# Cross-covariance attention folded into a gated FFN: an earlier load, smaller first folds, sums begun from 1e-9, and five trailing tiles

## Chip, cores, metric

One core of one Trainium2 chip. The metric is the device time of the kernel in microseconds (us), the median of several executions. Each kernel was also run once under the profiler; the span of an execution, from its first instruction to its last, is 1.7 to 2.2 us shorter than its timed duration. All executions used here are of the fast state, with a granted TensorE clock of 0.995 to 1.0, so no difference below is one of clock.

Engines in the profile: PE is TensorE, PEld its weight loads, DVE VectorE, ACT ScalarE, POOL GpSimd, SP SyncE. A name with q, such as SPq, is that engine's sequencer, which issues DMAs.

## The reference, cut

```python
# q, k, v: (4, 5824, 256) f32; tau = 1.0; w1, w2: (256, 1024); w3: (1024, 1024); w_out: (1024, 256)
qn = q / (norm(q, axis=1) + 1e-6)
kn = k / (norm(k, axis=1) + 1e-6)
a  = exp(kn.T @ qn / tau - max)              # 256 x 256 for each of 4 batches
a /= a.sum(-1) + 1e-9
x  = v @ a                                   # (4*5824, 256)
out = ((x @ w1) * (x @ w2)) @ w3 @ w_out     # (23296, 256) f32
```

## The kernel before

The kernel never forms `x`. For each batch it *folds* the softmax matrix into the weights, `Wf = a @ [w1 | w2]`, and once, for all batches, forms `W = w3 @ w_out`. What is left for every 512 rows of `v` and every 128 of the 1024 hidden columns (a "unit") is two products a and b of `v` with `Wf` (four 512-wide matmuls, on transposed `v`), a copy of a by ACT, a multiplication by DVE, and four 256-wide matmuls with `W`, which trail by two units. A batch has eleven chunks of 512 rows and a narrow one of 192 (128 rows, and 64 *left rows*). The q·k products G, squares, softmax and folds of the next batch are slipped between the units of the current one, at places that a clock in the program decides.

Batch 0 has no units to hide in: load of q and k, squares and G on TensorE, exponentials, sums and folds come before the first product.

```python
def sum_mm(c2):
    if c2 == 0:
        st["sum"] = psum.tile(...)
        ...
    for c1 in range(CT):
        nc.tensor.matmul(m[:, c1:c1+1], lhsT=st["e"][:, c2, c1*P:(c1+1)*P], rhs=ones_b,
                         start=(c1 == 0 and c2 == 0), stop=...)
    if c2 == CT - 1:
        nc.vector.tensor_scalar_add(rs, m[:, :CT], 1e-9)
        nc.vector.reciprocal(rs, rs)

def fold(i, ...):        # two 512-wide matmuls into a PSUM bank, evacuated with scale rs
    ...                  # by ACT (even i) or DVE (odd i)

# one later batch: (cost, time on the program's clock, work)
return (
    [(0.0, 0.0, norms), (0.0, 6.0, k_row)]      # norms: all-reduce over partitions, on GpSimd
    ...                                         # ACT and DVE: norms, scaling, exponentials
    + [(0.2, 15.5, sums)]
    + [(0.43, 16.5 + 0.85 * i, lambda i=i: fold(i)) for i in range(8)]
)

# loads while batch 0 is computed: (tensor, batch, piece, clock); t0..t1 spreads the q.k products
moves = [("v", 0, 3, 29.0), ("qk", 1, 0, 38.0), ..., ("v", 1, 2, 116.0), ("qk", 2, 0, 126.0)]
t0, t1 = 57.0, 115.5
```

All loads are issued by GpSimd and cast f32 to bf16 on the way.

## Time and profile before

| | before |
|---|---|
| median time (range) | 572.96 us (572.88 to 575.41), 3 runs |
| profile's span | 571.7 us |
| TensorE busy | 98% of the span |
| last large piece of k landed | 31.48 us |
| first product a | 40.69 us |

The table is read with the prediction below, which shows the page and the start. Columns of the timeline: start in us, duration, engine, line, operation, output and inputs, count, and in brackets the idle time before and its releaser.

Timeline of the kernel before, three lines from 47 to 167 us:

```profile
48.05 0.61 PE L132 MATMUL tr_I-620_621<-ident_b,v 128*128 128x128 bf16 x8
...
162.53 3.19 POOL L258 PARTITION_ALL_REDUCE tot<-acc  x1
...
166.12 0.42 ACT L279 ACTIVATE kr<-tot 128x256 f32<-128x256 f32 x1
```

The first is TensorE's transposing of v's second piece, which landed at 44.78: 3.3 us of slack. The all-reduce for batch 1 ends at 165.72, and ACT wants its result at 166.12: 0.4 us of slack. (In a second profile of the same kernel, b_again2 below, it is 164.54 and 165.61: 1.1 us.) No line has a wait, and so no wait told of the small margin.

Windows of the kernel before, 3 to 4 us (busy time of each engine with counts, then clock, DMA share, GB/s):

```profile
3.00:4.00 1.00, 1.00 (x4) 0.37 (x3) 0.00 (x0) 0.00 (x0) 1.00 (x3) 1.00 0.75 125
```

DMA is at 0.75 in the ramp, at 1.11 in each of the two microseconds after it.

### The profile page before, as it was taken

Reading aid. Unit: us, or ns where it says so; the run is one execution under the profiler, and the core shown is the slowest. Engines: PE = TensorE matmul, PEld = TensorE weight load, DVE = VectorE, ACT = ScalarE, POOL = GpSimd, SP = SyncE. Lnnn points to the kernel's source line nnn. Section 1 sums busy time; section 2 is a strip of 40 time slices with the busy share of each in tenths; the row PEclk is TensorE's granted clock in tenths of the full one; section 3 lists DMA queues with packets and bytes.
Section 4 is the critical chain, followed back from the end, with each engine's and each line's share of the span. In section 5 each row is a group of like instructions: output and inputs, shape, how many; then the busy total and the mean of one; then the engine's idle time right before and its main releaser. Section 6 shows DMA issues by size and latency. Waiting matters only on the chain.

```text
span 571.7 us, 10102 instructions
## 1 busy us (share of the span) xinstructions
PE 559.4 (98%) x3750; PEld 354.5 (62%) x3750; DVE 377.4 (66%) x612; ACT 337.7 (59%) x624; POOL 83.3 (15%) x164
## 2 busy tenths in 40 slices
PE   7789999999999999999999999999999999999997
PEld 4655576776666666666666666666665666666665
DVE  1047744788977567887776667778876656565564
ACT  0046644777856567776766567767766554454453
POOL 5250020303030111121030012031120000000000
PEclk9999999999999999999999999999999999999999
DMA  8999959869685697495661595665640325221011
GB/s 163 211 187 208 184 104 240 170 149 242 140 183 118 123 204 150 94 192 121 145 144 72 99 215 123 140 136 126 175 110 38 85 73 148 63 63 75 38 72 58
DMA packets 74560, 76.93 MB, mean 135 GB/s; under 512 B 54160, under 2 KB 58256, under 8 KB 74512
## 3 DMA queue, kind: packets, MB, share of 16 engines
q0 software_dynamic: 15504, 39.46, 39.3%
q1 hardware_dynamic: 58784, 36.64, 22.2%
q8 instruction: 29, 0.48, 0.3%
q10 hardware_dynamic: 224, 0.20, 0.1%
q14 instruction: 19, 0.16, 0.1%
HBM read 78.91 MB, written 23.86 MB: 180 GB/s over the span
## 4 chain that ended last, share of the span: by engine, by line
PE 92%; DMA 5%; DVE 1%; ACT 1%; POOL 1%; issue 0%; ACTq 0%; POOLq 0%
PE o L479 28%; PE a L438 27%; PE b L438 27%; PE G L188 5%; DMA k<-in_k_dram 5%; PE fold L349 2%; PE w L596 1%; ACT as L444 0%; ACT kr L279 0%; POOL k L109 0%; POOL q L109 0%; DVE abs L453 0%; PE sqk L221 0%; DVE vT L136 0%; DVE abs L455 0%
## 5 line engine op out<-in xcount | busy, mean ns | idle before, releaser
L453 DVE TENSOR_TENSOR abs<-as,b 128x512 bf16<-128x512 bf16 x336 | 230.5, 687 | 141.4 <-ACT as L444 130.3
L444 ACT CAST as<-a 128x512 bf16<-128x512 f32 (+1 forms) x384 | 216.1, 563 | 176.9 <-DVE abs L453 90.2
L438 PEld LDWEIGHTS <-Wf 128*128 128x128 bf16 x1536 | 149.2, 98 | 102.0 <-issue 1.9
L479 PE MATMUL o<-W_sb,abs 128*128 128x256 bf16 x1376 | 209.6, 273 | 0.1
L438 PE MATMUL a<-vT,Wf 128*128 128x512 bf16 x704 | 209.4, 379 | 0.2
L438 PE MATMUL b<-vT,Wf 128*128 128x512 bf16 x704 | 209.3, 379 | 0.0
L479 PEld LDWEIGHTS <-abs 128*128 128x128 bf16 x1376 | 134.5, 98 | 81.6 <-DVE abs L455 0.3
L197 DVE TENSOR_TENSOR acc<-acc,sq 128x1024 f32<-128x1024 f32 x66 | 80.4, 1219 | 0.4 <-ACT sq L185 0.3
L188 PE MATMUL G<-k,q 128*128 128x256 bf16 x276 | 49.9, 273 | 0.0
L185 ACT ACTIVATE sq<-q 128x512 f32<-128x512 bf16 x66 | 41.8, 634 | 0.0
L185 ACT ACTIVATE sq<-k 128x512 f32<-128x512 bf16 x66 | 41.6, 630 | 0.0
L426 POOL COPY gate_t<-abs 1x1 bf16<-1x1 bf16 x39 | 13.9, 355 | 167.7 <-DVE abs L453 167.0
L500 DVE COPY osb<-o 128x512 f32<-128x512 f32 x44 | 30.1, 685 | 0.7 <-PE o L479 0.7
L430 POOL COPY gate_t<-vT 1x1 bf16<-1x1 bf16 x17 | 4.4, 258 | 169.3 <-DMA vT<-v 134.0
L188 PEld LDWEIGHTS <-q 128*128 128x128 bf16 x276 | 27.0, 98 | 3.1
L499 ACT COPY osb<-o 128x512 f32<-128x512 f32 x44 | 25.8, 586 | 3.8 <-PE o L479 1.8
L279 ACT ACTIVATE kr<-row 128x256 f32<-128x256 f32 x1 | 0.4, 385 | 31.6 <-PE row L267 31.6
L109 POOL DMA_DIRECT2D q<-in_q_dram x29 | 15.7, 541 | 13.2 <-DMA k<-in_k_dram 6.0
L349 PE MATMUL fold<-w,e 128*128 128x512 bf16 x64 | 17.0, 380 | 0.5 <-DVE vT L136 0.4
L356 ACT ACTIVATE Wf<-fold,rs 128x512 bf16<-128x512 f32 x16 | 10.9, 688 | 8.1 <-PE fold L349 6.4
L244 DVE TENSOR_TENSOR dk<-sqk,ident 128x256 f32<-128x256 f32 x1 | 0.4, 425 | 21.3 <-PE sqk L221 21.3
L109 POOL DMA_DIRECT2D k<-in_k_dram x25 | 13.8, 551 | 3.7 <-DMA k<-in_k_dram 1.9
(89 smaller groups left out, 240.4 us busy)
## 6 DMA issues: line engine op xcount, KB each, us to landing
out_dram<-osb SPq DMA_DIRECT2D x44, 512.0 KB, 3.1
k<-in_k_dram POOLq DMA_DIRECT2D x19, 512.0 KB, 8.5
v<-in_v_dram POOLq DMA_DIRECT2D x19, 512.0 KB, 5.2
q<-in_q_dram POOLq DMA_DIRECT2D x18, 512.0 KB, 6.6
w_wout<-in_moe_w_dram POOLq DMA_DIRECT2D x1, 2048.0 KB, 23.6
k<-in_k_dram POOLq DMA_DIRECT2D x4, 320.0 KB, 9.9
v<-in_v_dram POOLq DMA_DIRECT2D x4, 320.0 KB, 5.4
q<-in_q_dram POOLq DMA_DIRECT2D x4, 256.0 KB, 12.0
```

What stands on the lines that cost most here:

```text
L109: nc.gpsimd.dma_start(out=pieces[nm, n, pi][:, lo:hi, :], in_=qk_main[nm, n][0][:, pi * PIECE + lo : pi * PIECE + hi, :])
L185: nc.scalar.activation(out=dst[:, :, part, :], in_=src[:, o : o + 2, :], func=AF.Square)
L188: nc.tensor.matmul(G[:, ct, :], lhsT=qt[:, i, ct * P : (ct + 1) * P], rhs=kt[:, i, :], start=(pr == 0 and part == 0 and ct == 0), stop=(pr ...
L197: nc.vector.tensor_add(accs[n], accs[n], sqs[0])
L349: nc.tensor.matmul(st["fold", i], lhsT=st["e"][:, c2, c1 * P : (c1 + 1) * P], rhs=w12[:, c2, w, h * 512 : (h + 1) * 512], start=(c2 == 0), ...
L426: nc.gpsimd.tensor_copy(gate_t, last_ab[0][:1, :1])
L438: nc.tensor.matmul(t[:, :n], lhsT=Wf[b][:, ct, w, j * P : (j + 1) * P], rhs=rhs_of(b, c, ct), start=(ct == 0), stop=(ct == CT - 1),)
L444: nc.scalar.copy(a_sb[:, :n], tiles[0][:, :n])
L453: nc.vector.tensor_mul(ab, a_sb, tiles[1])
L479: nc.tensor.matmul(tl[h][:, o, :], lhsT=lhsT, rhs=W_sb[:, j, :], start=(j == 0 and o == 0), stop=(j == FT - 1 and (small or o == 1)), skip ...
L499: nc.scalar.copy(o[:, 0:2, :], tl[0])
L500: nc.vector.tensor_copy(o[:, 2:4, :], tl[1])
```

## The change

Its intent: (1) the load of q and k starts earlier, with half of the first pieces over SP as f32, cast by DVE and ACT; (2) before the first product only a quarter of the fold is done, in 256-wide pieces (for this the weights come in three parts, behind v's first half); (3) the small add of 1e-9 on the way from sums to reciprocal goes, as the sums' bank is begun with 1e-9 by a tiny f32 matmul; (4) in later batches sums and folds come later on the clock and wider apart; (5) q and k of the next batch are loaded ahead of late v pieces, and their products come earlier; (6) in the very last chunk outputs trail by five units, left rows first.

```diff
+LAG_END = 5
+    tiny = consts.tile([1, P], F32)
+    nc.vector.memset(tiny, 1e-9)
 ...
+        def sum_start():
+            st["sum"] = psum.tile(...)
+            nc.tensor.matmul(st["sum"][:, :CT], lhsT=tiny, rhs=ones_pp[:1, :CT], start=True, stop=False, ...)
 ...
-                    start=(c1 == 0 and c2 == 0), stop=...
+                    start=False, stop=...
-                nc.vector.tensor_scalar_add(rs, m[:, :CT], 1e-9)
-                nc.vector.reciprocal(rs, rs)
+                nc.vector.reciprocal(rs, m[:, :CT])
 ...
+        def quarter_mm(lo, c1, c2):      # 256-wide folds of both weights, lo = 0 before the first product
+            ...
-            + [(0.2, 15.5, sums)]
-            + [(0.43, 16.5 + 0.85 * i, lambda i=i: fold(i)) for i in range(8)]
+            + [(0.2, 16.5, sums)]
+            + [(0.43, 17.5 + 1.1 * i, lambda i=i: fold(i)) for i in range(8)]
 ...
-        for s, lhsT in enumerate(lhs):
+        for s, lhsT in reversed(list(enumerate(lhs))) if small else enumerate(lhs):
 ...
-    busy(14)
-    load_piece("k", 0, 0, (half,))
-    load_piece("q", 0, 0, (half,))
+    busy(10)
+    for nm in "kq":
+        ...
+        nc.sync.dma_start(out=raw[nm], in_=qk_main[nm, 0][0][:, :half, :])
+        load_part(nm, 0, 0, half, PIECE)
 ...
-            for i in range(2):
-                at(1.5 + 0.6 * i, 0.43, soft0[5 + i])
+            at(0.5, 0.87, soft0[5])                       # second quarter
+            for i in range(4):
+                at((1.7, 2.6, 3.5, 3.9)[i], 0.43, soft0[7 + i])
 ...
-            moves = [("v", 0, 3, 29.0), ("qk", 1, 0, 38.0), ("qk", 1, 1, 43.0), ("v", 0, 4, 50.0), ("qk", 1, 2, 58.0)]
-            ...
-            t0, t1 = 57.0, 115.5
+            moves = [("qk", 1, 0, 29.0), ("v", 0, 3, 30.0), ("qk", 1, 1, 43.0), ("qk", 1, 2, 47.0), ("v", 0, 4, 53.0)]
+            ...
+            t0, t1 = 54.0, 113.0
 ...
-            t0, t1 = 16.0, 104.0
+            t0, t1 = 16.0, 98.0
 ...
-                while w_ready[0] and len(pend) > LAG and npop < 2:
+                lag = LAG_END if b == B - 1 and c == NCH - 1 else LAG
+                while w_ready[0] and len(pend) > lag and npop < 2:
```

## The prediction

> **What bounds the kernel now.** I read the page first, then the chain that ended last, the waits of TensorE, and the timeline of three places: the start, one stage where weights are folded, and the end.
>
> ```profile
> span 571.7 us, 10102 instructions
> PE 559.4 (98%) x3750; PEld 354.5 (62%) x3750; DVE 377.4 (66%) x612; ACT 337.7 (59%) x624; POOL 83.3 (15%) x164
> PE 92%; DMA 5%; DVE 1%; ACT 1%; POOL 1%; issue 0%; ACTq 0%; POOLq 0%
> L438 PE MATMUL a<-vT,Wf 128*128 128x512 bf16 x704 | 209.4, 379 | 0.2
> ```
>
> TensorE carries 92% of the chain and DMA 5%; the vector and scalar engines have a third of the span free. The 379 ns of one matmul is not its price: the timeline puts the start of each pair of 128x512 matmuls 0.43 us after the last pair, so one costs 0.216 us of TensorE, a 256-wide one 0.108. I took every matmul's start and subtracted columns/2400 us from the distance to the next. From 36 to 570 us this leaves 517.4 us of columns and 13.1 us of excess. Plain stretches have 0.16 us of excess in 10 us, some 8.5 in all. What is above that lies in few places: 0.5 us at 39 us (first folds), 3.3 us in the three later fold stages (1.0 near 175, 0.7 near 305, 1.6 near 440), 0.6 us at the end. Nothing between them can be won by waiting less. So three places are left: the load of q and k before the first product, the fold stages, the end.
>
> The start (timeline of 0 to 42 us; columns: start, duration, engine, line, operation, output and inputs, idle before and its releaser):
>
> ```profile
> 1.22 1.23 POOL L109 DMA_DIRECT2D k<-in_k_dram  x2 [0.78 <-POOLq L692]
> 31.53 0.84 PE L221 MATMUL sqk<-k 128*128 128x128 bf16 x12 [0.18 <-DMA k<-in_k_dram]
> 37.02 0.20 PE L328 MATMUL sum<-ones_b,e 128*128 128x1 bf16 x2 [1.25 <-ACT e L318]
> 39.82 1.04 PE L349 MATMUL fold<-w,e 128*128 128x512 bf16 x4 [0.35 <-DVE vT L136]
> 40.69 0.59 PE L438 MATMUL a<-vT,Wf 128*128 128x512 bf16 x2
> ```
>
> The first DMA is issued at 1.22 us and lands at 5.19; the last large piece of k lands at 31.48; from there a chain of squares, row sum, four activations, scaling and exponentials leads to the sums at 37.02, and folds fill TensorE until the first product at 40.69. In between DMA is the limit:
>
> ```profile
> 12.00:14.00 2.00, 1.08 (x14) 0.58 (x11) 0.00 (x0) 0.00 (x0) 0.34 (x1) 1.00 1.07 215
> ```
>
> DMA share is full at 215 GB/s written as bf16, that is 430 GB/s read as f32, with TensorE half idle (1.08 of 2.00). The later fold stage and the end:
>
> ```profile
> 438.29 1.65 PE L349 MATMUL fold<-w,e 128*128 128x512 bf16 x6
> 440.07 0.59 PE L438 MATMUL a<-vT,Wf 128*128 128x512 bf16 x2
> ...
> 567.45 0.28 PE L479 MATMUL o<-W_sb,abs 128*128 128x256 bf16 x1
> 568.60 0.53 ACTq L497 DMA_DIRECT2D out_dram<-oleft  x1
> ```
>
> Three folds in a row (1.29 us of columns) take 1.78 us until the next a, because each must be evacuated to free its bank. The last main output matmul starts at 567.45; copy, issue and landing take 4.2 us more.
>
> **What the Trainium skill says.** "TensorE: Matmul & The Clock Gate", section "Back-to-back issue gap", gives N/2.4 + 2.5 ns warm as the isolated gap, 216 ns for 512; the trace agrees with that (0.43 us for two), and not with the 131 ns that the section gives as sustained. "DMA: Bandwidth & Descriptors", section "Latency and other measured facts", gives the first byte of a transfer issued by SP or ACT as about 600 ns against about 1 us from GpSimd. The trace shows less of a difference: GpSimd's first issue at 1.22 has its first packet at 2.60 (1.38 us), ACT's store issued at 568.17 has its first at 569.51 (1.34 us). So I count only the earlier issue. The same page, section "SWDGE vs HWDGE vs iDMA", says that a cast during DMA needs GpSimd; the change accordingly loads f32 by SP and casts on DVE and ACT.
>
> **The change part by part.** The listing of both programs by engine gives the counts.
>
> *Start of the load.* Half of the first k and q pieces now come over SP as f32, which needs no descriptor work of GpSimd. ACT and DVE start at 0.72 and 0.80 us, so I take SP's first issue as 0.75 against 1.22: 0.5 us earlier; two queues filling at once should shorten the ramp (125 GB/s in the window of 3 to 4 us against 203 after), 0.2 more. The bytes read stay the same and the rate is the limit, so the whole load and the last k shift by 0.7 us. The two casts of 1024 columns (about 1 us each on idle engines) are ready before the pieces that arrived at 5.19 and 7.79 before. **-0.7.**
>
> *From the sums to the first product.* Before, 37.02 to 40.69 = 3.67 us. Now only the first quarter is folded: eight 256-wide matmuls, 0.87 us, and four sums, 0.2, so TensorE is done at about 38.1 on the old clock. The add of 1e-9 is gone, so the reciprocal is ready at about 38.0; ACT's and DVE's first 128x256 evacuations (about 0.4 us, as L313's 128x256) end at 38.5 to 38.7. First product at about 38.5 instead of 40.69: **-2.2.** The transposes of v (0.45) go into the idle time ahead of the exponentials, where a warm-up matmul is removed; v's half is loaded ahead of the weights, so it should be there.
>
> *Work put after the first product.* The second quarter (0.87) and four folds (1.73) now follow it, where two folds (0.86) followed: **+1.73**. ACT and DVE each have some 5.8 us of work in the 6.5 us that four products with these folds take. By hand, fold 7 waits 0.3 us for DVE to free its bank: **+0.4.**
>
> *Later fold stages.* Sums 1 us later after the exponentials, folds spaced 1.1 instead of 0.85. In the new order each of the last two batches has two folds to a unit of 0.86 + 0.43 us of products and outputs: ACT then has 0.59 + 0.69 and DVE 0.69 + 0.75 in 2.16 us. The bursts of three are gone. Against that stand three small f32 matmuls to start the sums, some 0.2 us each with their weight loads (the two-part f32 one at 5.94 us held TensorE 0.3 us), and for the second batch four folds remain in the narrow last chunk. I keep 1.5 of 3.3 us of excess: **-1.8.**
>
> *Moves of q, k and v, and earlier score products.* Before, v's fourth piece was transposed by 82.53 us and first used at some 107; TensorE never waited there. **0.**
>
> *End.* Before, from the first narrow product at 561.83 to the last main output at 567.45 is 5.62 us, where the columns alone are some 5.2. With five tiles trailing, TensorE issues the first three narrow products (0.33 us each) with no outputs between, but DVE needs 0.41 us a tile, which costs about 0.4 us; a bank copy of the chunk before now falls in the middle and costs 0.2 more. The waits at the very end vanish (0.3 before the last pair, 0.2 more before the pair at 563.98). **0, plus or minus 0.3.**
>
> Sum: -0.7 - 2.2 + 1.73 + 0.4 - 1.8 + 0 = -2.6 us. 572.96 - 2.6 = 570.4 us.
>
> **The rivals.** *The load gains more or nothing.* If a plain f32 load over SP is faster than a cast load, or fills the ramp wholly, the load ends 1.5 us earlier and the time is 569.5. If f32 into SBUF, twice the bytes written, is slower, or the two queues only share a rate that is full anyway, nothing is won: 571.1. The full DMA share speaks for the latter, the empty first 2.6 us for the former.
>
> *The first products starve.* ACT and DVE are close to full there, and the supply is close: with the same bytes ahead of them as before and the load 0.7 us earlier, the last weights (landed at 41.05) come at 40.3 and are used at about 42, v's second piece (44.78) at 44.1 and is used at about 45.5. If each of the first units waits 0.3 us, 1.2 us are lost: 571.6. For it: in the folds before, TensorE waited on DVE's vT and on w at 39.8. Against it: no unit between 41 and 50 us waited, with the same evacuations around.
>
> *The fold stages are cured wholly,* with f32 starts hidden in the array's queue: another 1.2 us, 569.2. *Reordered loads bring v late:* a product chunk of the first batch would wait for its transpose; each us late costs a us. The slack of over 20 us speaks against it.
>
> **Range and chances.** The terms err by 0.7 (load), 0.5 (first product), 0.5 (units after it), 0.7 (fold stages), 0.4 (end); in squares 1.3 us, and the median of three runs wanders by some tenths (572.88 to 575.41 here). For 8 in 10 I take 568.4 to 572.4. 2% is 11.5 us; all that lies outside the columns and the load does not add up to that on either side, so within 2% has 0.98.
>
> **What would show it.** Right: the last k lands near 30.8; first product at 37.3 to 38.3; excess in each later fold stage under 0.6 us above 0.16 per 10 us; the last narrow chunk takes 5.4 to 5.9 us. Wrong: waits of TensorE for DVE or ACT of over 0.5 us between 38 and 46; a wait for vT near 75 or 108 us; the last k still at 31.5; or a lower granted clock, which the page before gives as full throughout.

## The result

| | before | changed |
|---|---|---|
| median (range), 6 runs each, same rounds | 573.16 us (572.88 to 575.41) | 573.74 us (573.44 to 575.46) |
| ratio of fast runs | | 1.0011, 95% interval 0.9991 to 1.0030 |
| span of the profiled execution | 571.7 us | 573.3 us |

The same time, where I had expected 2.6 us less. A ratio here is the mean time of one kernel's fast runs over that of the other's in the same rounds, so not quite the ratio of the medians quoted. The profiled execution of the changed kernel took 575.46 us, the slowest of the six; the other five have spans of 571.3 to 572.3. Its trace therefore shows more waiting than the median run has, which is important below.

A part of the difference lies outside the span. Timed duration less span is 1.7 to 1.85 us in every run of the kernel before for which it is on record, and 2.1 to 2.2 us in all six of the changed kernel: 0.35 us that no trace here shows. By spans the two kernels are level (571.6 us is the median of the changed one here; the kernel before has 571.3 to 571.6 in the four later rounds). The new load alone (b_head2 below) has 2.0 to 2.1 us; a_sched2, which has it too, has 1.7 to 1.8. What makes it stays open.

The page of the changed kernel: span, busy shares, the chain by engine, and the group of product a.

```profile
span 573.3 us, 10143 instructions
PE 560.4 (98%) x3761; PEld 354.9 (62%) x3761; DVE 377.3 (66%) x610; ACT 339.3 (59%) x627; POOL 78.3 (14%) x164
PE 87%; DMA 7%; ACT 2%; POOL 1%; issue 1%; DVE 1%; POOLq 0%; ACTq 0%
L472 PE MATMUL a<-vT,Wf 128*128 128x512 bf16 x704 | 209.5, 379 | 2.1 <-ACT as L478 1.7
```

TensorE's share of the chain fell from 92% to 87% and DMA, ACT and issue gained. The idle time in front of product a rose from 0.2 to 2.1 us, put down to ACT.

Timeline of the changed kernel, the start:

```profile
0.73 0.40 SPq L551 DMA_DIRECT2D raw_k<-in_k_dram  x1
...
30.34 0.84 PE L224 MATMUL sqk<-k 128*128 128x128 bf16 x12 [0.19 <-DMA k<-in_k_dram]
...
35.99 0.20 PE L338 MATMUL sum<-ones_b,e 128*128 128x1 bf16 x2 [0.41 <-ACT e L321]
...
36.54 0.60 PE L385 MATMUL quarter<-w,e 128*128 128x256 bf16 x4
37.51 0.60 PE L472 MATMUL a<-vT,Wf 128*128 128x512 bf16 x2 [0.37 <-ACT Wf L394]
```

The first DMA is issued at 0.73, the last large k is used from 30.34 (31.53 before), and the first product starts at 37.51 against 40.69: the start did what it was meant to do. Windows of the changed kernel, 3 to 4 us:

```profile
3.00:4.00 1.00, 1.00 (x4) 0.38 (x3) 0.00 (x0) 0.00 (x0) 1.00 (x3) 1.00 1.00 410
```

The ramp is full (share 1.00, f32 written now). So the changed kernel is 3.2 us ahead at 37.5 us, and 1.6 us behind at the end of these two profiles. Where it is lost shows in marks along TensorE's program (us; "changed, edges moved back" is the run a_slack, in which no late data disturbs; the last column is the run a_oldfold; both are explained below):

| stretch | before | changed | changed, edges moved back | best (a_oldfold) |
|---|---|---|---|---|
| start to landing of last large k | 31.48 | 30.29 | 30.43 | 30.66 |
| to first sum matmul on e | 5.54 | 5.70 | 5.29 | 5.29 |
| to first product | 3.67 | 1.52 | 1.52 | 1.52 |
| batch 0: to first product of batch 1 | 141.42 | 146.28 | 144.22 | 143.27 |
| batch 1 | 132.76 | 132.91 | 132.90 | 132.41 |
| batch 2 | 133.21 | 132.96 | 132.96 | 132.34 |
| batch 3: to last output matmul | 119.49 | 119.57 | 119.57 | 119.49 |
| to the end | 4.08 | 4.09 | 4.08 | 3.93 |

Batch 0 is 4.9 us longer. 1.74 of it is the fold work put after the first product (from the columns of both instruction lists). The other 3.1 us had to be explained. The largest piece of it in this trace is at 163 us. Timeline of the changed kernel:

```profile
159.08 0.18 POOL L464 COPY gate_t<-vT 1x1 bf16<-1x1 bf16 x1 [9.88 <-DMA vT<-v]
...
160.45 3.19 POOL L261 PARTITION_ALL_REDUCE tot<-acc  x1
...
162.67 0.60 PE L513 MATMUL o<-W_sb,abs 128*128 128x256 bf16 x4
163.67 0.42 ACT L282 ACTIVATE kr<-tot 128x256 f32<-128x256 f32 x1 [3.24 <-POOL tot L261]
163.99 0.57 ACT L478 CAST as<-a 128x512 bf16<-128x512 f32 x1
...
164.61 0.59 PE L472 MATMUL a<-vT,Wf 128*128 128x512 bf16 x2 [1.34 <-ACT as L478]
```

Read from below: product a waited for ACT's copy, ACT had stood 3.24 us at `kr`, which needs the all-reduce, and the all-reduce began only at 160.45 though its input was ready at 153.95. GpSimd stood 9.88 us in a *gate*, the one-element copy that holds back the next v load until the last v piece is transposed, and the all-reduce stands behind that load in GpSimd's order. The chain of waits names ACT; the cause is GpSimd's order and the DMA behind it. The Trainium skill says where such a wait stands ("DMA: Bandwidth & Descriptors", section "Anatomy of one DMA — SWDGE (gpsimd) path": DMA engines do not wait on semaphores, a wait happens on the issuing sequencer before dispatch). In this trace it stands on the issuer too: 9.88 us on GpSimd, at the copy that the program puts ahead of the load.

The change brought this about itself: the q·k products end 2.5 us earlier on the clock, so ACT asks for `kr` earlier, while the gated v load moved by 2 us too and v's transposes land when DMA lets them.

### The profile page after: what moved, and what is told of

Same layout as the page of the kernel before. It is cut to its first block, busy times and chain, and to the rows that moved or that the text cites. A ratio compares the mean times of both kernels' runs of the same rounds, so it can differ in the third digit from the quotient of the medians.

```text
span 573.3 us, 10143 instructions
## 1 busy us (share of the span) xinstructions
PE 560.4 (98%) x3761; PEld 354.9 (62%) x3761; DVE 377.3 (66%) x610; ACT 339.3 (59%) x627; POOL 78.3 (14%) x164
## 4 chain that ended last, share of the span: by engine, by line
PE 87%; DMA 7%; ACT 2%; POOL 1%; issue 1%; DVE 1%; POOLq 0%; ACTq 0%
PE o L513 26%; PE b L472 26%; PE a L472 26%; PE G L191 5%; DMA k<-in_k_dram 3%; PE fold L359 2%; DMA q<-in_q_dram 2%; DMA vT<-v 2%; PE w L637 1%; ACT as L478 1%; DMA v<-in_v_dram 1%; POOL tot L261 1%; DVE abs L487 0%; ACT kr L282 0%; DVE s L316 0%
## 5 line engine op out<-in xcount | busy, mean ns | idle before, releaser
L460 POOL COPY gate_t<-abs 1x1 bf16<-1x1 bf16 x39 | 9.6, 246 | 173.0 <-DVE abs L487 172.2
L534 DVE COPY osb<-o 128x512 f32<-128x512 f32 x44 | 30.1, 685 | 0.8 <-PE o L513 0.7
L359 PE MATMUL fold<-w,e 128*128 128x512 bf16 x56 | 15.0, 379 | 0.2 <-ACT as L478 0.2
L487 DVE TENSOR_TENSOR abq<-as,b 128x512 bf16<-128x512 bf16 x16 | 10.8, 686 | 5.0 <-ACT as L478 4.5
```

The lines of the kernel that those rows point to most:

```text
L359: nc.tensor.matmul(m, lhsT=st["e"][:, c2, c1 * P : (c1 + 1) * P], rhs=w12[:, c2, w, lo:hi], start=(c2 == 0), stop=(c2 == CT - 1),)
L487: nc.vector.tensor_mul(ab, a_sb, tiles[1])
L534: nc.vector.tensor_copy(o[:, 2:4, :], tl[1])
```

## The experiments

Four theories of the missing 2.6 us. (A) The all-reduce wait of 163 us alone. (B) The tiny f32 matmul that starts the sums costs more than I allowed. (C) Several places where TensorE is now ahead of the data, of which the all-reduce is one. (D) The new end, or the new load, costs what was counted as nothing. Fifteen kernels ran. Four of them (b_again, b_head, a_sched, a_best1) had first been sent in a call that no chip took up, for no fault of theirs; they ran under labels ending in 2. Times below are this kernel's median against the kernel before in the same rounds.

### a_again: the changed kernel unaltered

```diff
 (no edit)
```

> The changed kernel once more, unaltered. Theory 1 (the gain is lost where GpSimd's all-reduce for batch 1 stands in its queue behind the wait for v's transpose): TensorE again has a gap of 0.5 us or more between an output matmul and the next product near 160 to 165 us, with ScalarE idle for the all-reduce before it; ratio to the kernel before 1.000 to 1.002. Rival 1 (the gap of 1.6 us belonged to the one profiled run, whose span was 573.3 us against 571.3 to 572.3 in the others): no such gap, span near 571.5, excess near 160 to 190 us about 1.6 us less than in the first profile, ratio the same.

573.86 us against 573.43; ratio 1.0006 (0.9991 to 1.0020); runs from 572.79 to 574.82. Span 572.2. The changed kernel's executions differ by 2 us among themselves. In this trace batch 0 takes 145.27 us, not 146.28, and the gap at 163 us is almost gone; another place waits, where TensorE transposes v's second piece. Timeline of a_again:

```profile
45.89 0.62 PE L135 MATMUL tr_I-615_616<-ident_b,v 128*128 128x128 bf16 x8 [0.87 <-DMA v<-in_v_dram]
```

The piece landed at 45.85, and TensorE lost 1.03 us there beyond its columns. So the waits move from place to place from one execution to the next, which speaks for C.

### a_reduce: the v load that stood ahead of the all-reduce put behind it

```diff
- ("v", 1, 2, 114.0)
+ ("v", 1, 2, 122.0)
```

> Only the load of v's third piece of batch 1, and the wait that goes with it, is moved from clock 114 to 122, behind the all-reduce in GpSimd's queue. Theory 1: the all-reduce ends near 157 us, ScalarE does not wait for it, the gaps near 163 and 171 us vanish, excess between 160 and 190 us falls from 4.4 to about 1.8 us, and the time falls by 1.5 to 2.8 us against the changed kernel (ratio to before 0.996 to 0.998). Rival 1 (rare): time changes by less than 0.5 us. Rival 2 (the stage is stalled by ScalarE's and VectorE's own load, not by the all-reduce): gaps of the same size stay in place.

573.53 us against 573.43; ratio 1.0002 (0.9989 to 1.0014). Span 571.5. The all-reduce ends at 157.56 and ACT asks at 160.59: the wait is gone, and the median is only 0.3 us below that of a_again in the same rounds, within the scatter of both. Theory A falls: the 1.6 us at 163 was one execution's.

### a_nostart: no tiny matmul, the add of 1e-9 back

```diff
-            nc.tensor.matmul(st["sum"][:, :CT], lhsT=tiny, rhs=ones_pp[:1, :CT], start=True, stop=False, ...)
-                    start=False,
+                    start=(c1 == 0 and c2 == 0),
-                nc.vector.reciprocal(rs, m[:, :CT])
+                nc.vector.tensor_scalar_add(rs, m[:, :CT], 1e-9)
+                nc.vector.reciprocal(rs, rs)
```

> The sums begin with start=True and the add of 1e-9 on VectorE again; no small f32 matmul. From the changed kernel's trace one of these costs TensorE 0.40 us (0.10 before, 0.13 within, 0.17 after), three times off the start. Theory: 1.0 to 1.2 us faster than the changed kernel, less up to 0.2 us for the first product, which waits for the add: 0.8 to 1.2 us in all. Rival (the gaps overlap with waits that come anyway): under 0.4 us.

571.76 us against 573.43; ratio 0.9974 (0.9960 to 0.9988). Span 569.4. This one part is worth some 2 us in the median (a_again: 573.86), late-data waits included. Batches 1 and 2 take 132.44 and 132.33 us, 0.5 and 0.6 less than with the start. What the start does is seen in the changed kernel's timeline (PE alone):

```profile
432.73 0.60 PE L513 MATMUL o<-W_sb,abs 128*128 128x256 bf16 x4
433.25 0.38 PE L329 MATMUL sum<-ones_pp,tiny 1*128 1x2 f32 x2
433.56 0.25 PE L338 MATMUL sum<-ones_b,e 128*128 128x1 bf16 x4
```

Four 256-wide matmuls are 0.43 us of columns, so the next matmul would start at 433.16; it starts at 433.25. The f32 matmul has two parts 0.13 us apart, and the sums start another 0.17 after the second: 0.09 + 0.13 + 0.17, about 0.40 us for two columns, where I had put 0.2. Theory B holds, in part: three starts are 1.2 us.

### a_lag2: the old end

```diff
-LAG_END = 5
+LAG_END = 2
-        for s, lhsT in reversed(list(enumerate(lhs))) if small else enumerate(lhs):
+        for s, lhsT in enumerate(lhs):
```

(and the order of the two multiplications of a narrow unit as before)

> The end as before: two tiles trailing, main rows first. From the first narrow product to the last main output it took 5.62 us before and 5.82 us (563.41 to 569.23) in the changed kernel. Theory: the end of the changed kernel gives nothing or costs 0.2 us, so this is 0.0 to 0.3 us faster. Rival (trailing helps, hidden by noise in one profile): 0.3 to 0.6 us slower.

572.98 us against 573.43; ratio 0.9993 (0.9980 to 1.0005), unclear by its interval. In the trace the narrow chunk up to the last output takes 5.75 us instead of 5.82, and from there to the end 3.91 instead of 4.09: the old end is 0.25 us shorter. The rest of the difference in the median lies within what the late-data waits do.

### b_lag5: the new end alone in the kernel before

```diff
+LAG_END = 5
-                while w_ready[0] and len(pend) > LAG and npop < 2:
+                while w_ready[0] and len(pend) > (LAG_END if b == B - 1 and c == NCH - 1 else LAG) and npop < 2:
```

(with the reversed output order)

> The kernel before with only the end of the changed kernel (five tiles trailing, left rows first). Theory: from the first narrow product to the last main output 5.82 us instead of 5.75 (to the last output matmul), the end after it 0.1 to 0.2 us longer: 0.1 to 0.4 us slower, within the noise. Rival: 0.3 to 0.6 us faster.

573.88 us against 573.32; ratio 1.0008 (0.9994 to 1.0021). In the trace 5.82 and 4.24 us against 5.75 and 4.08: 0.2 us longer. With a_lag2, the new end is a small loss, as far as 0.2 us can be told.

### b_again2: the kernel before unaltered

```diff
 (no edit)
```

> The kernel before once more, unaltered, for a second profile. Theory: the marks of the first profile come back within 0.3 us (last large k at 31.5, first product at 40.7, last main output at 567.6). Rival (the first profile was a lucky or unlucky one, as that of the changed kernel was by 1.7 us): the marks move by over 0.5 us, and part of the comparison is chance.

572.88 us against 573.10; ratio 0.9999 (0.9987 to 1.0011). Span 571.1, batches 141.4, 132.8, 133.2. The marks of the kernel before repeat within 0.05 us a batch, unlike those of the changed one. (In b_head2, next, batch 2 is 0.3 us shorter though only the load differs: a wait of TensorE in its narrow chunk has 0.16 us instead of 0.44. So a difference of 0.3 us in one batch need not come from an edit in it.)

### b_head2: the new load alone in the kernel before

```diff
-    load_piece("k", 0, 0, (half,))
-    load_piece("q", 0, 0, (half,))
+    nc.sync.dma_start(out=raw[nm], in_=...)     # k, then q: first halves as f32; cast by DVE, ACT
+    load_part(nm, 0, 0, half, PIECE)
```

> The kernel before with only the first halves of k and q over SP as f32, and ten warm-up matmuls instead of fourteen. Theory: the last large k lands at 30.3 to 30.7 as in the changed kernel, everything after shifts, 0.8 to 1.2 us faster (ratio 0.998 to 0.9985). Rival (the weights' landing then bounds the folds, since the queue of weights and v is the old one): k lands early but the first product gains under 0.5 us.

572.38 us against 573.10; the ratio 0.9997 (0.9974 to 1.0021) contains one run of 576.43 among 571.60 to 572.41. The marks of its trace stand 0.35 to 0.8 us earlier than b_again2's and 0.9 to 1.3 earlier than those of the first profile of the kernel before (last large k at 30.46). In the traces the new load keeps its gain when TensorE has slack to the data after it (the times alone do not resolve it); D falls for the load.

### a_sched2: the changed kernel with all of the old places on the clock

```diff
- moves = [("qk", 1, 0, 29.0), ("v", 0, 3, 30.0), ...]; t0, t1 = 54.0, 113.0;  later 16.0, 98.0
+ moves = [("v", 0, 3, 29.0), ("qk", 1, 0, 38.0), ...]; t0, t1 = 57.0, 115.5;  later 16.0, 104.0
- sums 16.5, folds 17.5 + 1.1 * i
+ sums 15.5, folds 16.5 + 0.85 * i
```

> The changed kernel with the loads, score products, sums and folds of all batches scheduled as in the kernel before (clock values only). Theory 2 (the new schedule cures part of the fold stages of batches 2 and 3, 1.2 us of waits, and costs 0.3 us in the stage of batch 1): 0.5 to 1.2 us slower than the changed kernel. Rival (the new schedule as a whole costs time, because the softmax of batch 1 now falls together with the late loads): 0.5 to 1.3 us faster than the changed kernel.

576.58 us against 573.10; ratio 1.0061 (1.0048 to 1.0073), the slowest kernel. Timeline of a_sched2:

```profile
139.52 0.38 PE L191 MATMUL G<-k,q 128*128 128x256 bf16 x2 [2.77 <-DMA k<-in_k_dram]
```

The old load order lets TensorE run into a piece of k, issued at 128.40 and landed at 139.48. So the faster start needs the reordered loads. Of the fold places this run says nothing, as the load order was undone with them; a_oldfold below takes them alone.

### a_best2: no start, no add, old end, folds of batch 1 earlier

```diff
- + [(0.2, 16.5, sums)]
- + [(0.43, 17.5 + 1.1 * i, ...)]
+ + [(0.2, 15.2 if n == 1 else 16.5, sums)]
+ + [(0.43, 15.7 + 1.05 * i if n == 1 else 17.5 + 1.1 * i, ...)]
```

(and the parts of a_nostart and a_lag2, without the add)

> The changed kernel without the f32 start of the sums and without the add of 1e-9 (which changes no bit of a sum above 0.01), with the end as before, and for batch 1 the sums 1.3 us and the folds 1.8 us earlier on the clock. Theory: the start of the sums costs 1.5 to 1.8 us, the end 0.3, the folds in the narrow chunk of batch 0 up to 0.5: 571.2 us, 2.0 to 2.6 us faster than the changed kernel, ratio to before 0.9955 to 0.9970. Rival for the folds: no gain from them, because ScalarE still does the exponentials then: as without the start of the sums, ratio 0.997 to 0.998.

573.80 us against 573.10; ratio 1.0008 (0.9996 to 1.0020): no gain, although its parts had gained alone. Its profiled execution was its fastest, 572.31, and even that loses 0.56 us beyond the columns at 63.87, ahead of the first `W` unit, whose transposed w3 landed at 64.59. That the slower runs have more such waits is argued, not shown.

Leaving out the add altogether, without a start, changes no result here: with tau = 1 each entry of the product of two normalized columns lies between -1 and 1, so a sum of 256 exponentials is over 90, and 1e-9 is lost in f32. (The 0.01 of the expectation should be 0.03; it makes no difference here.) All kernels without it were correct.

### a_slack: the changed kernel with the three edges moved back

```diff
-            at(7.0, 0.5, lambda: transpose_half_on_pe(0, 1, 0, True))
-            at(8.0, 0.5, lambda: transpose_half_on_pe(0, 1, 1, False))
+            at(10.0, 0.5, ...); at(11.0, 0.5, ...)
-                at(26.0 + 1.2 * jt, 0.87, lambda jt=jt: w_unit(jt))
+                at(29.0 + 1.2 * jt, 0.87, ...)
-            ("v", 1, 2, 114.0)
+            ("v", 1, 2, 122.0)
```

> The changed kernel with three uses of late data moved back: the last two transposes of v on TensorE from clock 7 and 8 to 10 and 11, the w units from 26 to 29, v's third piece of batch 1 behind the all-reduce (114 to 122). Theory 3 (the products that start 3 us earlier run into data that DMA delivers only some 1 us earlier: v near 45 us, the transposed w3 near 64, the all-reduce near 161; what comes late differs from one execution to the next): no gap over 0.2 us at these places, from the first product to the first of batch 1 143.6 to 144.3 us (144.5 to 146.3 in the changed kernel's two profiles and in the run with the all-reduce moved), time 0.5 to 1.2 us below the changed kernel's and runs within 1 us of each other. Rival (the waits only move to the next place, since the stream of loads is the limit through the whole first batch): same time as the changed kernel, gaps elsewhere.

573.28 us against 573.32; ratio 0.9995 (0.9983 to 1.0007). All runs lie between 573.10 and 573.39: a spread of 0.3 us instead of 2. Timeline of a_slack, the same instructions as shown above for the other kernels:

```profile
48.15 0.61 PE L135 MATMUL tr_I-652_653<-ident_b,v 128*128 128x128 bf16 x8
...
153.80 3.24 POOL L261 PARTITION_ALL_REDUCE tot<-acc  x1 [5.33 <-DVE acc L259]
...
160.07 0.42 ACT L282 ACTIVATE kr<-tot 128x256 f32<-128x256 f32 x1
```

The v piece landed at 44.52, 3.6 us ahead of use; the first transposed w3 at 64.19, used at 66.44; the all-reduce has 3 us of slack. Batch 0 takes 144.22 us and no wait for data is left in it. That supports C: TensorE had gained 3 us on a supply that gained 1 us at most. But its ratio is only 0.0016 below the changed kernel's (0.9 us; 0.5 by the medians), and the two intervals overlap, so C explains the scatter and perhaps a part; most of the missing 2.6 us lies elsewhere.

The rival, that the waits only move on, is true on a small scale. With the `W` units later, the fifth chunk begins at 73.4 us, where it had begun at 77.5 to 79, and the transposed third piece of v lands at 73.20. Two later runs of this order find it later and wait beyond the columns: a_slackold 0.21 us (landed 73.72), a_best3_rep 0.32 us (landed 73.67).

### a_best3 and a_best3_rep: a_slack without start and add, with the old end

```diff
 (a_slack's three moves)
-LAG_END = 5
+LAG_END = 2
-                nc.tensor.matmul(st["sum"][:, :CT], lhsT=tiny, ..., start=True, stop=False)
-                    start=False,
+                    start=(c1 == 0 and c2 == 0),
-        for s, lhsT in reversed(list(enumerate(lhs))) if small else enumerate(lhs):
+        for s, lhsT in enumerate(lhs):
```

> The same three moves, with no f32 start of the sums, no add, and the end as before; folds where the changed kernel has them. Theory 3 with the price of the sums' start: span 569.0 to 569.8 us, time 571.0 to 571.8 us, ratio to before 0.996 to 0.9975. Rival (waits move on): 572.5 or more, with gaps of 0.5 us and more elsewhere.

571.72 us against 573.32; ratio 0.9968 (0.9955 to 0.9980); spread 0.5 us. Batches 143.85, 132.42, 132.44. It was run again with the last two kernels:

> The best version again: 0.3% below the kernel before (ratio 0.995 to 0.998), some 571.7 us; stage from the first product to the next batch's 143.8 us, the next two 132.4 each.

571.78 us against 573.35; ratio 0.9965 (0.9940 to 0.9990). It repeats within 0.1 us in the median, within 0.4 in batch 0 of the trace (144.18, with the 0.32 us wait for v at 73.5). a_nostart, with the three edges where they were, has 571.76 us and no wait for data in its trace: how often the edges bite differs from call to call.

### b_sumstart: the start of the sums alone in the kernel before

```diff
+                if n > 0:
+                    nc.tensor.matmul(st["sum"][:, :CT], lhsT=tiny, rhs=ones_pp[:1, :CT], start=True, stop=False, ...)
-                nc.vector.tensor_scalar_add(rs, m[:, :CT], 1e-9)
-                nc.vector.reciprocal(rs, rs)
+                nc.vector.reciprocal(rs, m[:, :CT])      # batch 0 keeps the add
```

> The kernel before with only the f32 start of the sums in batches 1 to 3 (and no add there). Theory: 0.4 to 0.55 us in each of three stages, 1.2 to 1.6 us slower (ratio 1.002 to 1.003). Rival (in the kernel before the wait for the exponentials hides it): under 0.5 us slower.

573.61 us against 573.32; ratio 1.0000 (0.9988 to 1.0012). By the traces batches 0, 1 and 2 change by +0.33, +0.12 and -0.17 us: 0.3 in all, where three starts of 0.40 would cost 1.2. The rest comes back: by the missing add, or because a start goes into a wait that was there (the rival). This run cannot part the two, as it changes both. One place shows how: the three folds in a row near 438 us that the prediction had shown. Timeline of the kernel before, ahead of them:

```profile
436.50 0.59 PE L349 MATMUL fold<-w,e 128*128 128x512 bf16 x2
...
437.69 0.15 DVE L334 TENSOR_SCALAR rs<-sum 128x2 f32<-128x2 f32 x1
437.87 0.17 DVE L335 RECIPROCAL rs<-rs 128x2 f32<-128x2 f32 x1
438.13 0.69 ACT L356 ACTIVATE Wf<-fold,rs 128x512 bf16<-128x512 f32 x1 [1.19 <-DVE rs L335]
```

and of b_sumstart, TensorE:

```profile
439.11 1.46 PE L356 MATMUL fold<-w,e 128*128 128x512 bf16 x6
440.44 0.59 PE L445 MATMUL a<-vT,Wf 128*128 128x512 bf16 x2
```

In the kernel before, ACT waited 1.19 us for `rs` with the first fold (436.50) standing in its bank and the copy of the next unit's a behind it in ACT's order, so banks came free late, and the burst took 1.78 us. In b_sumstart the same burst at the same place takes 1.33 us, and its columns are 1.29. It had not waited for evacuations as such; it had waited for the reciprocal. Two shifts make up the 0.45 us: measured from the end of DVE's products before it (437.76 and 438.33), `rs` is ready 0.20 us earlier without the add (0.08 instead of 0.28 after them), and the burst comes 0.25 us later, as the start holds TensorE up. So the add's part here is about 0.2 us, an estimate; no run takes out the add alone.

### a_oldfold and a_slackold: sums and folds at the old places, without and with the start

```diff
-            + [(0.2, 16.5, sums)]
-            + [(0.43, 17.5 + 1.1 * i, lambda i=i: fold(i)) for i in range(8)]
+            + [(0.2, 15.5, sums)]
+            + [(0.43, 16.5 + 0.85 * i, lambda i=i: fold(i)) for i in range(8)]
```

(a_oldfold: made on a_best3; a_slackold: made on a_slack)

> The best version with sums and folds of the later batches at the old places (15.5; 16.5 + 0.85 i). If moving the folds wins nothing (theory: the burst excess was mostly not the folds'), the three stages keep 143.8, 132.4 and 132.4 us and the time is within 0.2 us of the best version. If the move wins what I had predicted less the start's true cost (rival: about 1.2 us for all three), the stages are longer by 0.3 to 0.6 us each and the time is about 572.9.

571.09 us against 573.35; ratio 0.9954 (0.9931 to 0.9976). Span 568.9. Runs from 570.80 to 571.35, where a_best3_rep in the same rounds has 571.61 to 572.00. It is the fastest kernel. Both expectations were wrong, and in sign: moving the folds later had not won little, it had *lost* 0.7 us. Batches 143.27, 132.41, 132.34 against 144.18, 132.42, 132.44: nearly all of it in the first, where 0.32 of the 0.91 us is the wait for v at 73.5 (against a_best3, without it, 0.58).

Timeline of a_best3_rep in the narrow chunk of batch 0:

```profile
178.93 0.59 PE L356 MATMUL fold<-w,e 128*128 128x512 bf16 x2 [0.17 <-ACT as L475]
...
180.30 0.33 PE L469 MATMUL b<-vTt,Wf 128*128 128x192 bf16 x2 [0.17 <-ACT Wf L363]
```

and of a_oldfold in the wide chunk before it:

```profile
171.27 1.46 PE L356 MATMUL fold<-w,e 128*128 128x512 bf16 x6
172.57 0.59 PE L469 MATMUL a<-vT,Wf 128*128 128x512 bf16 x2
```

Spread by 1.1, five of the eight folds fall into the narrow chunk, where a unit has half the TensorE time for its evacuations, and TensorE waits for ACT. At the old places six folds are done in the wide chunks, three in a row, and the burst takes 1.30 us for 1.29 of columns: bursts of three cost nothing there.

> The changed kernel with its late-data edges moved back, start of the sums kept, folds at the old places. If the old places hide the start in a wait that is there anyway (as the kernel before with a start showed, +0.3 us in all), it is as fast as a_oldfold within 0.4 us. If not, it is 1.5 us slower than a_oldfold, as the changed kernel is slower than the one without the start.

572.41 us against 573.35; ratio 0.9976 (0.9953 to 0.9998). It is 1.32 us slower than a_oldfold, of which the end is 0.22 (5.81 and 4.09 against 5.75 and 3.93) and the three batches 0.32, 0.49 and 0.37: 1.18. The 0.21 us that a_slackold waits for v at 73.5 is in the first, so the starts cost 0.11, 0.49 and 0.37, about 1.0. In batch 0 a start does go into a wait: TensorE loses 0.27 us behind the sums in a_oldfold and nothing there in a_slackold. In the other two it costs the 0.4 that the single timeline shows.

## Why the prediction was wrong, point by point

*Start of the load, -0.7.* Right. The last large k landed at 30.1 to 30.7 in the changed kernels, 31.3 to 31.5 in the two runs of the kernel before: about -0.9, and the ramp is full as argued. From there to the sums another 0.25 us was won (5.54 to 5.29 in an undisturbed run) that I had not foreseen. (Two more runs with the old load, b_lag5 and b_sumstart, have 31.49 and 32.14.) One reading was wrong: the packet at 569.51 belongs to SP's store issued at 568.36 (1.15 us), and ACT's store of 568.17 had its first packet at 569.05 (0.88 us). SP's first load in the changed kernel took 1.03 us to its first packet, GpSimd's in the kernel before 1.38, so there was a difference to count. Not only the issue is earlier: the first packet moved from 2.60 to 1.76, 0.84 us, about what the load gained. Of the rivals, neither extreme of the load came.

*From the sums to the first product, -2.2.* Right. 3.15 to 3.71 us became 1.52, -1.6 to -2.2 (-2.0 against the mean of the two profiles of the kernel before); first product at 37.51, in the range named.

*Work put after the first product, +1.73 and +0.4.* The work is 1.74 by columns. The wait of TensorE between 38 and 44 us is only about 0.1: 0.08 ahead of the last fold. (a_slack seems to lose another 0.22 at 42.96; there one of the fold's two matmul records is missing.)

*The rival "the first products starve".* It came, in a wider form than I had written. I had asked whether the units up to 50 us would wait, and counted slack only there. TensorE came 3 us earlier. In the two profiles of the changed kernel v's second piece landed at 44.28 and 45.85 (44.78 before) and the first transposed w3 at 63.79 and 64.88 (63.73 before). So the 3.3 us of slack that each had became 0.7 us in one profile and a wait in the other for v, and 0.3 and 0.2 us for w3; the all-reduce had 0.4 us to begin with. In the traces it costs 0.3 to 2 us, different from run to run; a_slack, which moves the three edges, is 0.5 us faster in the median than the changed kernel (0.9 by the ratios, whose intervals overlap) and scatters by 0.3.

***"Later fold stages", -1.8: the step that failed.*** I wrote: "I keep 1.5 of 3.3 us of excess". Free of late data (a_slack), the three stages became about 0.9 us *longer*: batch 0 by 144.22 - 141.42 - 1.74 - 0.1 = +0.96, batch 1 by +0.14, batch 2 by -0.25. Three terms make this up, each from a pair of kernels (the start's pair differs in the end too, which lies outside these batches):

| term | I had | measured | from |
|---|---|---|---|
| three starts of the sums | +0.6 | +1.0 | a_slackold against a_oldfold: 0.11 + 0.49 + 0.37, the wait for v taken off |
| later, wider places of the folds | the cure, with the rest -2.4 | +1.1 | a_slack against a_slackold: 0.84 + 0.00 + 0.25, the wait for v taken off (without the start, a_best3 and its repeat against a_oldfold: 0.7 each, likewise) |
| all else: no add, other places of G and loads | in the line above | -1.2 | a_oldfold against before, with the moved work and 0.1 taken off: 0.0 - 0.35 - 0.87 |

The sum is +0.9. The reason is a misread line. From the burst of 1.78 us at 438 us I concluded that three folds in a row wait for their banks, and took the wider spacing for the cure. In the same trace the other four bursts of three do not wait. Timeline of the kernel before:

```profile
305.01 1.46 PE L349 MATMUL fold<-w,e 128*128 128x512 bf16 x6
306.30 0.59 PE L438 MATMUL a<-vT,Wf 128*128 128x512 bf16 x2
...
307.60 1.46 PE L349 MATMUL fold<-w,e 128*128 128x512 bf16 x6
308.90 0.33 PE L438 MATMUL a<-vTt,Wf 128*128 128x192 bf16 x2
```

1.29 and 1.30 us for 1.29 of columns. At 305.01 `rs` was ready only at 305.20, after the burst had begun, and still it did not wait. The burst at 438 us differs in that a single fold had gone ahead of it, at 436.50: ACT stood at that fold for `rs` (ready at 438.04), with a unit's copy behind it. Of the 3.3 us of excess only about 0.6 lie between a fold and what follows it, 0.5 of that in this one burst; another 0.6 lie ahead of three single folds in batch 0's narrow chunk, and the rest is not at folds. So there was no 1.5 to win from bursts. And this one's wait went in b_sumstart at the old spacing, by the earlier `rs` and the later TensorE together.

Of the -1.2 the add is a part that was not taken out alone. b_sumstart gives up to 0.9 for it (+0.28 with three starts of up to 0.4), less what of the starts went into waits. At the new places it is worth nothing that can be read: a_nostart, with the add, has 132.44 and 132.33 us in batches 1 and 2, a_best3, without it, 132.42 and 132.44. Of the 0.87 us of batch 2 the traces put 0.45 at sums and folds (436 to 440 us) and 0.39 in the narrow chunk behind them, where 0.3 moves even between two runs in which that stage is the same (b_head2 against before).

*Moves of q, k and v, 0.* Right for the wrong reason. I argued from the slack of v, 20 us; what the moves do is keep k ahead of its earlier use: with the old order TensorE waits 2.8 us for a k piece (a_sched2). And v's third piece, which I had not looked at, was left without slack once the `W` units had moved: the wait for vT near 75 us that I had named as a sign of being wrong came in two of the variants, a_slackold and a_best3_rep, with 0.21 and 0.32 us.

*End, 0 ± 0.3.* Right: +0.07 to the last output in the changed kernel, and about 0.2 us to be had by the old end.

Sum with measured terms, without late data: -0.9 - 0.25 - 2.0 + 1.74 + 0.1 + 0.9 + 0.1 = -0.3 us; the median span of a_slack is 571.2 us against 571.5 of the kernel before in the same rounds. The edges and the 0.35 us outside the span take that back and a little more: 573.74 against 573.16.

Left open: how "all else" divides between the add and the other places of G and loads; what the 0.35 us outside the span is; how much each of the three edges costs in the median, since their waits move from run to run; and a gap of about 0.3 us behind batch 1's exponentials near 170 us that is in most changed kernels.

## What to carry to other kernels

When a change brings the critical engine forward, list the slack (landing against use) of every later input over the whole span, not just of the ones near by: a place without a wait may have 0.4 us left, and 3.3 us were too little here. Before taking a burst's excess for a bank limit, look at the other bursts of the same size in the same trace, and at what the evacuating engine waited for. Count the records before a gap of one matmul's length is called a wait. And price a small matmul by the distance from the matmul before it to the one after it: 0.4 us for two columns here, more than the VectorE add that it replaced was worth.

## What the Trainium skill lacked or had wrong

- "DMA: Bandwidth & Descriptors", section "Latency and other measured facts": the first byte of a transfer issued by SP or ACT at about 600 ns against about 1 us from GpSimd. Here, from the start of the issue to the first packet, SP's first load took 1.03 us (0.73 to 1.76), ACT's first store in the kernel before 0.88, and GpSimd's first load there 1.38: all longer, with about the page's difference between them. In the changed kernel GpSimd's loads, issued from 1.22 us beside SP's two, had their first packets only at 4.81, between the landings of SP's pieces (4.58 and 5.81); why stays open.
- "TensorE: Matmul & The Clock Gate", section "Back-to-back issue gap": 131 ns sustained for a 512-wide matmul. The traces of all kernels here show 216 ns (pairs 0.43 us apart), the figure that the section gives for an isolated one.
- No page gives the price of a small f32 matmul between bf16 ones: 0.40 us here (two parts 0.13 us apart, 0.17 to the next, 0.10 ahead).
- No page gives the time of a partition all-reduce of 128x512 f32: 3.19 to 3.24 us on GpSimd in the records.
